# Four edits to a fused attention and MLP kernel: QK tiles cut at chunk borders, whole-tile stores, reciprocals on VectorE, and a new TensorE order

## The chip, the core and the metric

The kernel runs on one core of a Trainium2 chip. TensorE (PE) multiplies, VectorE (DVE) and ScalarE (ACT) empty the PSUM banks and do the elementwise work, GpSimd (POOL) does small elementwise work and issues the loads of inputs, and SyncE (SP) issues the DMAs that move data inside the chip's on-core memory and the stores of results. The metric is the device time of one execution in microseconds (us), here of three runs of the kernel before, and of one execution that the profiler recorded.

## The reference

Inputs are q, k, v of shape 8 batches x 12 heads x 448 tokens x 64, two 12 x 12 matrices that mix heads, and the two MLP weights (768 x 2048 and 2048 x 768).

```python
scores = scale * np.matmul(q, k.transpose(0, 1, 3, 2))
scores = np.einsum('bhij,hg->bgij', scores, w_pre)
attn = np.exp(scores - np.max(scores, axis=-1, keepdims=True))
attn = attn / (np.sum(attn, axis=-1, keepdims=True) + 1e-09)
attn = np.einsum('bhij,hg->bgij', attn, w_post)
x = np.matmul(attn, v)            # heads side by side: 3584 x 768
h = np.maximum(x @ w_in, 0.0)
return h * h @ w_out
```

## The kernel before

**Chunks and tiles.** Mixing heads contracts over heads, so for one token all 12 heads have to lie on partitions. A chunk is 10 tokens of one batch with 12 heads, 120 rows, in two groups of 60 (5 tokens each). A batch has 45 chunks (the last one has 8 tokens and is moved as two pieces of 4). The scores q k^T are made in QK tiles of many tokens, one head per PSUM bank (`emit_QK`, line 955), emptied into `stage` (two slots, tokens on partitions), and carried from there by DMAs on SP into `dring`, a ring of 16 chunk slots with heads and tokens on partitions (`emit_rel`, line 1023). A chunk that crosses the border of two QK tiles needs two of these DMAs. QK tiles are 128, 128, 128 and 64 tokens; the tile of 64 is multiplied for two pairs of heads at once, so that it needs 3 TensorE units and not 6.

For the first 30 chunks of batch 0 there is a direct way without `stage`: q is spread with zeros in `qz`, and units `spr` write scores with heads and tokens already on partitions. The other 148 tokens of batch 0 are two QK tiles.

**Softmax.** Units `pre` mix the heads of a pair of chunks (`emit_pre`, line 1045). ACT takes the exponent, with the sum of each row in `rowsum` (line 1094). Then `rec` (line 1109 on) writes the reciprocals of a pair's row sums to `rinv`: on DVE with the reciprocal instruction for the first five pairs, on POOL as a power of minus one for the other 179 (line 1117, `minus1` is its exponent). `fold` multiplies them into the second mixing matrix (`wk2s`, line 1127, on POOL after the first five pairs). Units `post` (line 1159) mix the exponents with `wk2s` into the transposed second scores, which DVE or ACT copies to `a2t`. Units `avq` and `av` multiply with v (lines 1216, 1237) into `xt`. The no-max form of softmax is checked at the end: after the last exponent, DVE tests all row sums, SP turns the answer round by a DMA, and a flag is made (`t_flag`).

**MLP.** Units `h` (`emit_F1`, line 1275) multiply by w_in, ACT or DVE takes the positive part, DVE squares into `h2t`. Units `o` (`emit_F2`, line 1406) multiply 128 result rows by w_out. The rows are emptied into `osb` (two slots) and stored by DMAs on SP (line 1473): one per piece of `pieces_of`, two pieces of 64 rows for nearly all tiles, since the rows of `h2t` are even and odd groups of tokens that lie apart in the output. The last two tiles store half rows each as soon as it is there (`emit_last`, line 1366).

**What sets the order.** The program is written out whole by a planner (`_Plan`). The order of TensorE's units is the string ORDER, one character a unit: the position of the character in CODES, divided by ten, gives the form (0, 1, 2), and the remainder the stream (0 transposes, 1 QK, 2 pre, 3 post, 4 av, 5 direct units, 6 and 7 `h`, 8 and 9 `o`) from which the next unit is taken. The form is how the 128 x 128 array is split: `row` (two halves of 64 rows at once), `quad` (four 64 x 64 blocks), `full`, `cols`, `c32`. Units `h` and `o` can run in any of row, full and quad; in `row` and `quad` both banks of a pair are filled together over two units, in `full` one after the other. The other four engines' tasks are put in order by the planner from its costs: FETCH (an instruction block's arrival), DMA times, and a cost for each task. An eviction that may run on ACT or DVE goes to the one that the planner expects to be done first. Each engine then runs its list in order and waits on semaphores.

**The end.** `emit_engine` (line 1624): each engine runs its list, waits for the flag, loads it into a register (line 1631) and branches (line 1632): when a row sum was out of range everything is done again with the maximum taken off. SP waits for its stores (`final`, line 1574) only behind that branch.

Of the kernel before, what the change touches and what calls it, by code (L numbers as in the profile page):

```python
# [7 lines left out]
ALU = mybir.AluOpType  # L8
DT = mybir.dt
# [3 lines left out]
ACT = "act"  # L13
DVE = "dve"
POOL = "pool"
SP = "sp"
# [3 lines left out]
MODE_SWITCH = 100.0  # L20
ACT_BIAS = 14.5
BLOCK = 256
FETCH = (2700.0, 2300.0, 1500.0)
EVENTS = {"tr": 0.12, "qk": 0.72, "di": 0.2, "sp": 0.3, "po": 0.61, "pr": 1.1, "av": 0.43, "o0": 0.43}
DMA_START = {"move": 2590.0, "load": 2640.0, "big": 1680.0}
DMA_AHEAD = 1600.0
DMA_END = {"move": 1450.0, "load": 1300.0}
INF = float("inf")
CODES = "0123456789abcdefghijklmnopqrst"
ORDER = (  # L30
    "0000511100551155555555555555555c2155555035bcb02515525353c2c5155c1531333355c2555c355332c0"
    "240443c4b200gh1111h62b3g33hqc31cgc3h2b3hgh3bbbch3633r3gb42444223g1h72qgqb2733g1r12q713h3"
    "6b2673722392003t122j33t2b282bi338333s04202444bb002gqbb28311i313s111s322gh2227hqh3613q1hr"
    "3363q2422444br2br631q1731h613q32h0220gh22qg373r3c38212i3s333814144420022ghh20028118111i1"
    "33s339b22j31t22193229119313t3319242444312q2bq227373163c3631731h2020q1g2br2h236333q20b0r2"
    "r20038318311i33184bb42244229c19311t133t118222833i313s242444232q2b623713733631g12r2br2006"
    "33q33rb17q200262r217293c3t331t2200jc181118133s311842244422391319313t13392422444222838333"
    "i311i31qb2b62qb2622h73733373q1b6rb00h2q0202q22h700239331911j11193182238318331s2424442228"
    "1s311i333814244413bq22g2rb2r23631q32r2br23633g31r002h2633q733r024044412tb2j0209bb2t23811"
    "381138333s11t22jb2922t23831s33i1318b4244422bq2bqb27337631q33731r2q21q2r22h1633673373bs22"  # L40
    "842i2i244422383833s333s22qr6r22293933t33tq4q444hghh6gq7g6hrghisrggh7hg7giqishhjjijtsttsj"
    "j"
)


# [327 lines left out]
def bass_talking_heads_attention__then__ffn_squared_relu_kernel(  # L373
# [10 lines left out]
    B, H, S, D = q.shape  # L384
# [4 lines left out]
    NR = CH * H  # L389
    NCH = -(-S // CH)  # L390
    IT = 128
    ND = 30
    NE = 6
    NQ0 = 2
    QT0 = tuple((CH * (ND + x * (NCH - ND) // NQ0),
                 min(S, CH * (ND + (x + 1) * (NCH - ND) // NQ0))) for x in range(NQ0))
    QT = tuple((i, min(S, i + IT)) for i in range(0, S, IT))
    NP = H // 2
    PJ = 64
    NT = S // PJ  # L400
# [15 lines left out]
    with ExitStack() as es:  # L416
        def sb(name, shape, dtype):
            return es.enter_context(nc.sbuf_tensor(name, list(shape), dtype))
# [29 lines left out]
        goods = sb("goods", [1, 128], DT.float32)  # L448
        flag = sb("flag", [1, 1], DT.int32)
        rinv = sb("rinv", [128, NPS, 1], DT.float32)  # L450
        minus1 = sb("minus1", [128, 2, 1], DT.float32)
        sb("align", [128, 64], DT.uint8)
        w_in_sb = sb("w_in_sb", [128, NFT, FF], DT.bfloat16)
        w_out_sb = sb("w_out_sb", [128, NFFT, F], DT.bfloat16)
# [38 lines left out]
        def program(guard):  # L493
# [9 lines left out]
            def add(name, engine, fn, deps, cost, prio, mode=None, group=None, instrs=0):  # L503
                return plan.add(name, engine, fn, deps, cost, prio, "ctr", 1, mode, group=group,
                                instrs=instrs)
# [28 lines left out]
            def fn_init(eng, en):  # L534
                eng.memset(mask[:, :, :], 1.0)
                eng.memset(wk1[:, :], 0.0)
                eng.memset(wrep[:, :], 0.0)
                eng.memset(wrepf[:, :], 0.0)
                eng.memset(maskf[:, :], 0.0)
                eng.memset(wkf[:, :, :], 0.0)  # L540
                eng.memset(wk2b[:, :, :], 0.0)
                eng.memset(rowsum[:, NCP - 1::NCP, :], 1.0)
                eng.memset(minus1[:, :, :], -1.0)
                return eng.memset(ident[:, :], 0.0)

            t_init = add("init", DVE, fn_init, [], {DVE: (950.0, 1050.0)}, -3e6)
# [476 lines left out]
            def emit_rel(b, c, n, r0, d0, nv):  # L1023
                g = b * NCP + c
                slot = g % NDS
                sem = sem_dsx[c // (IT // CH) - 1] if d0 else sem_dsl[slot]

                def fn(eng, en):
                    o = R0 + d0 * H
                    eng.dma_start(dring[o:o + nv * H, slot, :],  # L1030
                                  stage[r0:r0 + nv, n % 2, :, :]).then_inc(sem.handle, 16)

                t = plan.add("rel%d_%d_%d" % (b, c, d0), SP, fn, sev_of[n],
                             {SP: (1000.0, 0.0)}, g * 1.0, sem, 16,
                             dma=("move", 10.0 + 73.3 * nv, 54.0))
                rel.setdefault(g, []).append(t)
                rel_of[n].append(t)
# [48 lines left out]
            def after_pre(g, t_pre, gr, x):  # L1086
# [26 lines left out]
                p0 = g0 % NPS  # L1113

                def fn_rec(eng, en):
                    if en == POOL:
                        return eng.tensor_tensor(rinv[:, p0:p0 + n, :], rowsum[:, g0:g0 + n, :],  # L1117
                                                 minus1[:, 0:n, :], ALU.pow)
                    return eng.reciprocal(rinv[:, p0:p0 + n, :], rowsum[:, g0:g0 + n, :])

                t_rec = add("rec%d_%d" % (b, c), DVE if g < 10 else POOL, fn_rec,
                            [exp_of[g0], t_exp] + old_users(g),
                            {DVE: (82.0, 160.0), POOL: (120.0, 180.0)}, b * 1000.0 - 900 + c)

                def fn_fold(eng, en):
                    i0 = wk2b[:, :, :].rearrange("p a b -> p (a b)").unsqueeze(1)
# [279 lines left out]
            def emit_F2(b, tile, s, s_F):  # L1406
# [58 lines left out]
                    if hh == 0:  # L1465
                        f.early.append(t_oe)
                pieces = pieces_of(b, tile)

                o_free[s] = []
                for x, (p0, n_p, row, step) in enumerate(pieces):  # L1470
                    def fn_od(eng, en, p0=p0, n_p=n_p, row=row, step=step):
                        dst = bass.AP(out.tensor, row * F, [[step * F, n_p], [1, F]])
                        eng.dma_start(dst, osb[p0:p0 + n_p, s, :]).then_inc(sem_out[s].handle, 16)

                    o_free[s].append(plan.add("odma%d_%d_%d" % (b, tile, x), SP, fn_od, evs,
                                              {SP: (720.0, 0.0)}, b * 1000.0 + 710, sem_out[s], 16,
                                              dma=("move", 50.0 + 12.0 * n_p, 200.0)))
                odmas.extend(o_free[s])


# [55 lines left out]
            if not guard:  # L1536
                inside = stage[:, 1, 0:2, :].rearrange("p a b -> p (a b)")[:, 0:B * NCP]
                i_ = rowsum[:, :, :].rearrange("p a b -> p (a b)")
                last_exp = [t for g, t in exp_of.items() if g >= B * NCP - NCP]
                used = [t for ts in rel.values() for t in ts]  # L1540

                def fn_in(eng, en):
                    return eng.tensor_scalar(inside, i_, 1e30, None, op0=ALU.is_lt)

                def fn_both(eng, en):
                    return eng.scalar_tensor_tensor(inside, i_, 1e-30, inside, op0=ALU.is_gt,
                                                    op1=ALU.mult)

                def fn_least(eng, en):
                    return eng.tensor_reduce(good[:, :], inside, AX.X, ALU.min)  # L1550

                def fn_turn(eng, en):
                    eng.dma_start(goods[0:1, :], good[:, 0:1]).then_inc(sem_good.handle, 16)

                def fn_flag(eng, en):
                    return eng.tensor_reduce(flag[:, :], goods[:, :], AX.X, ALU.min)

                t_in = add("good0", DVE, fn_in, list(exp_of.values()) + used,
                           {DVE: (450.0, 550.0)}, 1e8)
                t_in = add("good1", DVE, fn_both, [t_in], {DVE: (450.0, 550.0)}, 1e8)  # L1560
                t_in = add("good2", DVE, fn_least, [t_in], {DVE: (450.0, 550.0)}, 1e8)
                t_turn = plan.add("turn", SP, fn_turn, [t_in], {SP: (780.0, 2800.0)}, 1e8, sem_good, 16)
                t_flag = add("flag", DVE, fn_flag, [t_turn], {DVE: (200.0, 300.0)}, 1e8)

            for g, ts in rel.items():
                for t in ts:
# [57 lines left out]
        def emit_engine(eng_name, eng):  # L1624
            tasks = fast[eng_name]
            k = len(tasks)
            while k and tasks[k - 1].name == "final":
                k -= 1
            emit_tasks(eng_name, eng, tasks[:k], fast_waits)
            eng.wait_ge(t_flag.sem.handle, t_flag.semval)  # L1630
            fine = eng.value_load(flag[0:1, 0:1])
            with eng.If(fine == 0):
                emit_tasks(eng_name, eng, tasks[k:], fast_waits)
                for s_, v_ in reached:
                    eng.wait_ge(s_.handle, v_)
                emit_tasks(eng_name, eng, slow[eng_name], slow_waits)
            if k < len(tasks):
                with eng.Else():
                    emit_tasks(eng_name, eng, tasks[k:], fast_waits)

        with nc.Block() as block:
            @block.tensor
# [46 lines left out]
```

## Time and profile before

| | |
|---|---|
| three runs | 538.87, 530.79, 534.45 us; median 534.45 |
| the profiled execution | 531.75 us, of which its span is 530.1 |
| PE busy | 504.9 us, 95% of the span |
| ACT busy | 429.9 us, 81% |
| DVE busy | 387.7 us, 73% |
| POOL busy | 292.6 us, 55% |
| matmuls | 10519 |

The span runs from the first to the last instruction. "Busy" counts the time in which at least one instruction of an engine was under way; matmuls overlap, and the time from the start of one unit to the start of the next says more of TensorE than the duration that is printed. In a list by time, a row has the start, the time from start to end of a merged run of like instructions, engine, line, operation, tiles, and the count. In a list of groups, the columns behind the bar are the busy time, the mean duration in ns, and the idle time of the engine just before them with what ended it. In a list of waits a row reads: engine and line, the engine and line that it waited for, total us, times, longest.

### The profile page before, as it was taken

What the parts mean: (1) busy time and instruction counts of PE and PEld (TensorE: products, weight loads), DVE (VectorE), ACT (ScalarE), POOL (GpSimd) and SP (SyncE); (2) the same over time, 40 slices, a digit from 0 to 9 for tenths busy, and PEclk for the clock granted to TensorE, in tenths of its full rate; (3) what the DMA queues carried; (4) which work ended last, traced back from release to release, by engine and by line L of the source; (5) the groups of instructions that cost most, each with busy time, mean ns of one, the idle gap of its engine ahead of it and who ended that gap; (6) DMA issues with size and microseconds to landing.
All of it is one profiled execution on the core that took longest, in us unless ns stands there. A gap on an engine that the chain in (4) does not pass through costs nothing.

```text
span 530.1 us, 24988 instructions
## 1 busy us (share of the span) xinstructions
PE 504.9 (95%) x10519; PEld 329.4 (62%) x10519; DVE 387.7 (73%) x816; ACT 429.9 (81%) x1223; POOL 292.6 (55%) x524
## 2 busy tenths in 40 slices
PE   8999999999999999999899989999999999999994
PEld 4446776668765655666566655566666665678862
DVE  7898987889886699867787667776888668555400
ACT  5999989889978798888798878978978878977420
POOL 9847788527944597258752576416964445442000
PEclk9999999999999999999999999999999999999998
DMA  9999999646965799458954699536992567531022
GB/s 165 197 201 172 181 192 183 140 96 138 180 147 117 158 167 185 101 113 155 176 115 96 126 196 151 119 64 146 181 176 55 124 139 145 113 93 35 1 57 70
DMA packets 81811, 71.10 MB, mean 134 GB/s; under 512 B 13610, under 2 KB 78234, under 8 KB 81690
## 3 DMA queue, kind: packets, MB, share of 16 engines
q1 hardware_dynamic: 48138, 46.62, 36.1%
q0 software_dynamic: 33392, 22.59, 31.3%
q8 instruction: 86, 1.41, 1.1%
q14 instruction: 35, 0.29, 0.2%
q10 hardware_dynamic: 160, 0.20, 0.1%
HBM read 45.63 MB, written 11.01 MB: 107 GB/s over the span
## 4 chain that ended last, share of the span: by engine, by line
PE 72%; ACT 15%; POOL 7%; DVE 2%; issue 2%; DMA 1%; ACTq 0%; POOLq 0%
PE ps L1435 23%; PE ps L1296 13%; PE ps L1288 7%; PE ps L1159 7%; ACT pring L1094 6%; PE ps L1069 5%; PE ps L1237 5%; PE ps L985 4%; ACT stage L524 4%; POOL rinv L1117 3%; PE ps L1375 2%; PE ps L1427 2%; ACT dring L524 1%; POOL wk2s L1127 1%; PE ps L975 1%
## 5 line engine op out<-in xcount | busy, mean ns | idle before, releaser
L1117 POOL TENSOR_TENSOR rinv<-rowsum,minus 128x2 f32<-128x2 f32 (+1 forms) x179 | 126.1, 706 | 174.7 <-ACT pring L1094 173.9
L1094 ACT ACTIVATE pring<-ps 128x448 bf16<-128x448 f32 x360 | 192.3, 562 | 12.0 <-PE ps L1069 9.4
L525 DVE CAST a2t<-ps 128x480 bf16<-128x480 f32 (+1 forms) x205 | 124.8, 641 | 31.6 <-PE ps L1159 30.6
L1435 PE MATMUL ps<-w_out_sb,h2t 64*128 64x384 bf16 (+1 forms) x1728 | 141.4, 323 | 0.5 <-issue 0.4
L525 DVE CAST stage<-ps 128x448 bf16<-128x448 f32 (+1 forms) x193 | 115.0, 617 | 25.8 <-PE ps L985 15.1
L1296 PE MATMUL ps<-xt,w_in_sb 64*64 64x448 bf16 (+4 forms) x1872 | 121.0, 327 | 1.8 <-issue 1.2
L524 ACT ACTIVATE a2t<-ps 128x480 bf16<-128x480 f32 (+1 forms) x163 | 87.6, 581 | 22.5 <-PE ps L1159 21.7
L1435 PEld LDWEIGHTS ps<-w_out_sb,h2t 64*128 64x128 bf16 (+1 forms) x1728 | 74.6, 97 | 45.1 <-issue 1.9
L524 ACT ACTIVATE stage<-ps 128x448 bf16<-128x448 f32 (+1 forms) x167 | 87.0, 549 | 14.3 <-PE ps L985 9.6
L1296 PEld LDWEIGHTS ps<-xt,w_in_sb 64*64 64x64 bf16 (+1 forms) x1872 | 65.0, 102 | 34.5 <-issue 2.5
L1094 ACT ACTIVATION_READ_ACCUMULATOR pring<-ps 128x1 f32 x360 | 81.6, 227 | 0.0
L1127 POOL TENSOR_TENSOR wk2s<-wk2b,rinv 128x120 bf16<-128x120 bf16 (+1 forms) x179 | 70.7, 396 | 12.4
L1159 PEld LDWEIGHTS ps<-wk2s,pring 60*128 60x128 bf16 x2880 | 56.6, 93 | 31.9 <-DVE a2t L525 4.8
L1159 PE MATMUL ps<-wk2s,pring 60*128 60x60 bf16 x2880 | 64.8, 187 | 6.9 <-POOL wk2s L1127 4.2
L1343 DVE TENSOR_TENSOR h2t<-h1t 128x448 bf16<-128x448 bf16 (+2 forms) x176 | 53.3, 331 | 23.3 <-ACT h1t L1333 22.5
L1069 PE MATMUL ps<-dring,wk 64*64 64x448 bf16 (+1 forms) x622 | 54.5, 359 | 2.6 <-ACT h1t L1333 0.9
L1333 ACT ACTIVATE h1t<-ps 128x448 bf16<-128x448 f32 (+2 forms) x93 | 40.4, 439 | 14.4 <-PE ps L1288 5.9
L1334 DVE TENSOR_SCALAR h1t<-ps 128x448 bf16<-128x448 f32 (+2 forms) x83 | 41.3, 505 | 11.4 <-PE ps L1296 8.4
L1288 PE MATMUL ps<-xt,w_in_sb 128*128 128x220 bf16 (+2 forms) x420 | 47.4, 265 | 0.2
L1288 PEld LDWEIGHTS ps<-xt,w_in_sb 128*128 128x128 bf16 x420 | 38.2, 98 | 7.3 <-ACT pring L1094 0.9
L985 PE MATMUL ps<-qkt 64*128 64x448 bf16 (+1 forms) x288 | 39.5, 353 | 1.4 <-DVE a2t L525 0.8
L738 POOL DMA_DIRECT2D vraw<-in_v_dram x54 | 34.3, 640 | 0.0
(76 smaller groups left out, 434.2 us busy)
## 6 DMA issues: line engine op xcount, KB each, us to landing
dring<-stage SPq DMA_DIRECT2D x301, 105.0 KB
out_dram<-osb SPq DMA_DIRECT2D x45, 192.0 KB, 3.6
qraw<-in_q_dram POOLq DMA_DIRECT2D x42, 112.0 KB, 5.0
kraw<-in_k_dram POOLq DMA_DIRECT2D x42, 112.0 KB, 5.1
w_in_sb<-in_moe_w_in_dram POOLq DMA_DIRECT2D x8, 384.0 KB, 10.2
w_out_sb<-in_moe_w_out_dram POOLq DMA_DIRECT2D x8, 384.0 KB, 8.9
vraw<-in_v_dram POOLq DMA_DIRECT2D x21, 128.0 KB
vraw<-in_v_dram POOLq DMA_DIRECT2D x21, 96.0 KB
```

The lines of the kernel that those rows point to most:

```text
L524: return eng.activation(o, i_, AF.Copy)
L525: return eng.tensor_copy(o, i_)
L985: r_ = eng.matmul(ps[y * w:(y + 1) * w, g.banks[x], 0:S], qkt[r0:r0 + 64, pb, p + y, 0, i0:i0 + w], qkt[r0:r0 + 64, pb, p + y, 1, :], star ...
L1069: r_ = eng.matmul(ps[64 * y:64 * y + 64, gr.banks[x], 0:S], wk1[64 * x:64 * x + 64 - R0 * x, 64:128], dring[64 * x:64 * x + 64 - R0 * x, ( ...
L1094: return eng.activation(pring[:, pr, 0:S], ps[:, gr.banks[x], 0:S], AF.Exp, accum_out=rowsum[:, g, :])
L1117: return eng.tensor_tensor(rinv[:, p0:p0 + n, :], rowsum[:, g0:g0 + n, :], minus1[:, 0:n, :], ALU.pow)
L1127: return eng.tensor_tensor(wk2s[:, p0:p0 + n, :], i0.to_broadcast([128, n, PR]), rinv[:, p0:p0 + n, :].to_broadcast([128, n, PR]), ALU.mult)
L1159: r_ = eng.matmul(ps[:, gr.banks[x], o0:o0 + PR], pring[64 * x:64 * x + PR, pr + y, j0:j0 + 2 * PJ], wk2s[64 * x:64 * x + PR, pr + y, :], ...
L1288: r_ = eng.matmul(ps[:, g.banks[ph], 0:n], w_in_sb[:, ft, t * 128:(t + 1) * 128], xt[:, ft, c0:c1], start=(ft == 0), stop=(ft == NFT - 1))
L1296: r_ = eng.matmul(ps[z:z + w, g.banks[x], 0:n], w_in_sb[64 * y:64 * y + 64, ft, t * 128 + z:t * 128 + z + w], xt[64 * y:64 * y + 64, ft, c ...
L1343: return eng.tensor_tensor(h2t[:, t16, o0:o0 + n], h1t[:, s, 0:n], h1t[:, s, 0:n], ALU.mult)
L1435: r_ = eng.matmul(ps[z:z + w, g.banks[hh], 0:FH], h2t[64 * y:64 * y + 64, t16, col + z:col + z + w], w_out_sb[64 * y:64 * y + 64, t16, hh ...
```

## The change

1. QK tiles of batches 1 to 7 are 120, 120, 120 and 88 tokens. Each of the four is made by 6 units (the last one computes 128 rows, of which 88 are used). No chunk crosses a border, so each chunk is one DMA. In batch 0 the direct way takes 32 chunks and one QK tile of 128 tokens the rest.
2. In batches 1 to 7, two pieces of a result tile are stored by one DMA with a three-level address; the tile that joins two batches, those of batch 0 and the last two stay as they were.
3. All reciprocals are on DVE; `minus1` is gone.
4. ACT and SP take the flag and the branch in the middle of their lists, as soon as the flag is there (tasks `turnact` and `turnsp`), and have what follows written twice, behind each side of the branch.
5. The planner's costs for an instruction block (4.0 us whatever the DMAs do), for a DMA's end and for SP's issue are others, and ORDER is a new string of 986 characters in place of 969.

```diff
-FETCH = (2700.0, 2300.0, 1500.0)
+FETCH = (4000.0, 0.0, 0.0)
...
-DMA_END = {"move": 1450.0, "load": 1300.0}
+DMA_END = {"move": 1700.0, "load": 1300.0}
...
 ORDER = (
-    "0000511100551155555555555555555c2155555035bcb02515525353c2c5155c1531333355c2555c355332c0"
...
+    "0051100555500555555155555555555222555555553155311cc002c53002255531c5352335555c3525155333300"
...
-    ND = 30
+    ND = 32
     NE = 6
-    NQ0 = 2
+    NQ0 = 1
...
-    QT = tuple((i, min(S, i + IT)) for i in range(0, S, IT))
+    QT = tuple((i, min(S, i + 120)) for i in range(0, 360, 120)) + ((360, S),)
...
-                             {SP: (1000.0, 0.0)}, g * 1.0, sem, 16,
+                             {SP: (950.0, 0.0)}, g * 1.0, sem, 16,
...
                 def fn_rec(eng, en):
-                    if en == POOL:
-                        return eng.tensor_tensor(rinv[:, p0:p0 + n, :], rowsum[:, g0:g0 + n, :],
-                                                 minus1[:, 0:n, :], ALU.pow)
                     return eng.reciprocal(rinv[:, p0:p0 + n, :], rowsum[:, g0:g0 + n, :])
 
-                t_rec = add("rec%d_%d" % (b, c), DVE if g < 10 else POOL, fn_rec,
-                            [exp_of[g0], t_exp] + old_users(g),
-                            {DVE: (82.0, 160.0), POOL: (120.0, 180.0)}, b * 1000.0 - 900 + c)
+                t_rec = add("rec%d_%d" % (b, c), DVE, fn_rec, [exp_of[g0], t_exp] + old_users(g),
+                            {DVE: (82.0, 160.0)}, b * 1000.0 - 900 + c)
...
-
+                whole = b and not (b % 2 and tile == 3)
                 o_free[s] = []
-                for x, (p0, n_p, row, step) in enumerate(pieces):
+                for x, (p0, n_p, row, step) in enumerate(pieces[:1] if whole else pieces):
                     def fn_od(eng, en, p0=p0, n_p=n_p, row=row, step=step):
-                        dst = bass.AP(out.tensor, row * F, [[step * F, n_p], [1, F]])
-                        eng.dma_start(dst, osb[p0:p0 + n_p, s, :]).then_inc(sem_out[s].handle, 16)
+                        if whole:
+                            dst = bass.AP(out.tensor, row * F, [[F, 2], [step * F, n_p], [1, F]])
+                            i_ = osb[:, s, :]
+                        else:
+                            dst = bass.AP(out.tensor, row * F, [[step * F, n_p], [1, F]])
+                            i_ = osb[p0:p0 + n_p, s, :]
+                        eng.dma_start(dst, i_).then_inc(sem_out[s].handle, 16)
...
+                for en in (ACT, SP):
+                    plan.add("turn" + en, en, None, [t_flag], {en: (3600.0, 3600.0)}, -1e8)
...
-            while k and tasks[k - 1].name == "final":
-                k -= 1
+            for i, t in enumerate(tasks):
+                if t.name == "turn" + eng_name:
+                    k = i
+            rest = tasks[k + 1:]
             emit_tasks(eng_name, eng, tasks[:k], fast_waits)
             eng.wait_ge(t_flag.sem.handle, t_flag.semval)
             fine = eng.value_load(flag[0:1, 0:1])
             with eng.If(fine == 0):
-                emit_tasks(eng_name, eng, tasks[k:], fast_waits)
+                emit_tasks(eng_name, eng, rest, fast_waits)
                 for s_, v_ in reached:
                     eng.wait_ge(s_.handle, v_)
                 emit_tasks(eng_name, eng, slow[eng_name], slow_waits)
-            if k < len(tasks):
+            if rest:
                 with eng.Else():
-                    emit_tasks(eng_name, eng, tasks[k:], fast_waits)
+                    emit_tasks(eng_name, eng, rest, fast_waits)
```

More of the change, by code (lines that the diff above doesn't have):

```diff
@@ L30 @@
 ORDER = (
-    "0000511100551155555555555555555c2155555035bcb02515525353c2c5155c1531333355c2555c355332c0"
[L32 to L42, printed above, removed]
+    "0051100555500555555155555555222555555553155311cc002c53002255531c5352335555c3525155333300"
+    "5242111431244322g32qh331rg3b3h612bbhgh2b3r2226hg333g2h2424443c3h611g13gr111h622g337h7332"
+    "hqg0220hg3b2911j111t333j2040244224381001i111i13c83bbqbqbc3831c82238c12i373h33gh22237h6q3"
+    "32g4244314b22hghqb2bg7133gh22b00i3c3s333bg2r1b1h2b671363q32020g2h2gr3373r200bb8b2b8bb424"
+    "4332c8c3i111s331811224239323j323tt24b2441134332hbb22g319333t22b9020bj317bbb6g33r2002h22h"
+    "336bb002g331hbbbg222ghqb2bh333ibb28bb22j3339242444333s111832bsb2bi42244432s223823g313gbb"
+    "002t113j2b2g2373373373r0022ghbb002gbbb6133g22267b2h333h332tb2b9bbb92424442j2381183138133"
+    "814244b239222j39313931831182422i118200263363731r30022ghb0220hb2bq116333636131q2r2bhbrb22"
+    "r4244439133j24244421j113j3383s22281i138133s2200i122s6113637331r31gb22hg220000h6313q17131"
+    "h32q2b62rb2h42444223913j1139133933s2ib2s284b24443831s33i1812t2bt2b29b2j236333g711371bq22"
+    "6qb2g2713r3733h32q42q2hri22444333siigj9h2222rgt383i33833i49hg6g444ghhg7iqhg7qgsghig8qrhg"
+    "rhhhhjqsjij99ts89j"
 )
@@ L450, in bass_talking_heads_attention__then__ffn_squared_relu_kernel @@
         rinv = sb("rinv", [128, NPS, 1], DT.float32)
-        minus1 = sb("minus1", [128, 2, 1], DT.float32)
         sb("align", [128, 64], DT.uint8)
@@ L542, in fn_init @@
                 eng.memset(rowsum[:, NCP - 1::NCP, :], 1.0)
-                eng.memset(minus1[:, :, :], -1.0)
                 return eng.memset(ident[:, :], 0.0)
@@ L1467, in emit_F2 @@
                 pieces = pieces_of(b, tile)
+                whole = b and not (b % 2 and tile == 3)
                 o_free[s] = []
-                for x, (p0, n_p, row, step) in enumerate(pieces):
+                for x, (p0, n_p, row, step) in enumerate(pieces[:1] if whole else pieces):
                     def fn_od(eng, en, p0=p0, n_p=n_p, row=row, step=step):
-                        dst = bass.AP(out.tensor, row * F, [[step * F, n_p], [1, F]])
-                        eng.dma_start(dst, osb[p0:p0 + n_p, s, :]).then_inc(sem_out[s].handle, 16)
+                        if whole:
[5 more added lines that the diff above has]
+                        eng.dma_start(dst, i_).then_inc(sem_out[s].handle, 16)
                     o_free[s].append(plan.add("odma%d_%d_%d" % (b, tile, x), SP, fn_od, evs,
-                                              {SP: (720.0, 0.0)}, b * 1000.0 + 710, sem_out[s], 16,
-                                              dma=("move", 50.0 + 12.0 * n_p, 200.0)))
+                                              {SP: (900.0 if whole else 720.0, 0.0)},
+                                              b * 1000.0 + 710, sem_out[s], 16,
+                                              dma=("move", 50.0 + 12.0 * n_p * (2 if whole else 1),
+                                                   200.0)))
                 odmas.extend(o_free[s])
```

## The prediction

> **What bounds the kernel now.** I read the page's busy times and chain first, then TensorE's list by time, then the waits.
>
> ```profile
> span 530.1 us, 24988 instructions
> ...
> PE 504.9 (95%) x10519; PEld 329.4 (62%) x10519; DVE 387.7 (73%) x816; ACT 429.9 (81%) x1223; POOL 292.6 (55%) x524
> ...
> PE 72%; ACT 15%; POOL 7%; DVE 2%; issue 2%; DMA 1%; ACTq 0%; POOLq 0%
> ```
>
> TensorE is busy for 95% of the span and is 72% of the chain that ended last. So the end moves with what TensorE has to do and with the gaps between its units. The list by time, PE alone, shows both:
>
> ```profile
> 111.71 0.39 PE L1159 MATMUL ps<-wk2s,pring 60*128 60x60 bf16 x16
> 111.93 0.35 PE L985 MATMUL ps<-qkt 64*128 64x448 bf16 x2
> 112.13 0.39 PE L1159 MATMUL ps<-wk2s,pring 60*128 60x60 bf16 x16
> 112.35 1.46 PE L1435 MATMUL ps<-w_out_sb,h2t 64*128 64x384 bf16 x16
> 113.65 0.73 PE L985 MATMUL ps<-qkt 64*128 64x448 bf16 x6
> 114.22 1.46 PE L1435 MATMUL ps<-w_out_sb,h2t 64*128 64x384 bf16 x16
> 115.52 0.39 PE L1159 MATMUL ps<-wk2s,pring 60*128 60x60 bf16 x16
> 115.83 0.57 PE L1069 MATMUL ps<-dring,wk 64*64 64x448 bf16 x8
> 116.34 1.30 PE L1288 MATMUL ps<-xt,w_in_sb 128*128 128x220 bf16 x12
> 117.57 0.76 PE L1069 MATMUL ps<-dring,wk 64*64 64x448 bf16 x10
> ```
>
> Take differences of starts. Where the form stays `row` (111.71 to 115.52), a `post` takes 0.22, an `o` unit 1.30, three QK units 0.57, so 0.19 for a pass of 448 columns, and nothing lies between. Where the form changes, about 0.1 comes on top: 0.31 for a `post` of 0.22 (row, then quad), 0.51 for two `pre`, each one such pass (quad, then full), and 1.23 for two full `h` units that should take 1.13 (then quad). Where that 1.13 is from, and the two ends of TensorE's work:
>
> ```profile
> 194.66 1.30 PE L1296 MATMUL ps<-xt,w_in_sb 64*128 64x448 bf16 x12
> 195.79 0.39 PE L1159 MATMUL ps<-wk2s,pring 60*128 60x60 bf16 x16
> ...
> 5.29 0.95 PE L833 MATMUL ps<-ident,qraw 64*64 64x64 bf16 x28
> ...
> 514.39 7.96 PE L1375 MATMUL ps<-w_out_sb,h2t 128*128 128x384 bf16 x48
> ```
>
> An `h` unit of 448 tokens takes 1.13; two full ones of 220 tokens stream about as many columns. Now the account. Units: 112 `o` x 1.30 = 145.6; 128 `h` of 448 tokens' worth x 1.137 = 145.5; 434 passes of 448 columns in QK, `pre` and direct units x 0.19 = 82.5; `post`, 180 pairs' worth, x 0.22 = 40; attention times v, per half batch 22 passes of some 224 columns, half of 0.19 each, so 2.08, x 16 = 33.3; transposes, 48 units of 0.24 (the last two rows under rival B), 12. Together 459. Walking ORDER character by character, each stream's units in the order in which they are made, I count 216 changes of form: x 0.11 = 23.8. The first real unit starts at 5.3 and the last ends at 514.39 + 7.96 = 522.4. What is left, **34 us** (522.4 - 5.3 - 459 - 23.8), is TensorE standing still. 7.7 us of the span lie behind its end, and 1.65 outside the span (531.75 - 530.1).
>
> **The change, part by part.**
>
> *Work.* Seven batches have 24 QK units in place of 21, batch 0 has 6 in place of 12: 15 more. Two more direct chunks are 4 passes, and the other forms of `pre` take one off. 18 x 0.19 = **+3.4**.
>
> *Form.* The new ORDER has 307 changes, 91 more, since 148 of the `h` and `o` units are `full` against 78: 91 x 0.11 = **+10.0**. It also has 9826 matmuls in place of 10502 (10519 less 17 warm-ups), because `full` does with one matmul what `row` does with two.
>
> *Standing still.* 13.4 us have to be won back from the 34. What the waits name:
>
> ```profile
> PE ps L1159 <- POOL wk2s L1127: 4.2, 5, 1.3
> ...
> PEld ps L1159 <- POOL wk2s L1127: 1.2, 2, 0.7
> ...
> POOL rinv L1117 <- ACT pring L1094: 173.9, 62, 8.2
> ```
>
> ```profile
> L1117 POOL TENSOR_TENSOR rinv<-rowsum,minus 128x2 f32<-128x2 f32 (+1 forms) x179 | 126.1, 706 | 174.7 <-ACT pring L1094 173.9
> ...
> L1119 DVE RECIPROCAL rinv<-rowsum 128x2 f32<-128x2 f32 x5 | 0.8, 152 | 0.0
> ```
>
> `post` waits 5.4 for POOL. A pair's reciprocals take 706 ns there and 152 on DVE, so the way from exponent to `post` is 0.55 shorter 179 times, and POOL falls from 293 to 167 busy. I take the 5.4 as gone; what is late next is the eviction of `post`'s banks. DVE gets 179 x 0.152 = 27.2.
>
> ```profile
> L525 DVE CAST stage<-ps 128x448 bf16<-128x448 f32 (+1 forms) x193 | 115.0, 617 | 25.8 <-PE ps L985 15.1
> L524 ACT ACTIVATE stage<-ps 128x448 bf16<-128x448 f32 (+1 forms) x167 | 87.0, 549 | 14.3 <-PE ps L985 9.6
> ```
>
> Evictions: the last tile has 12 before and after (64 partitions then, 128 now, the same row); batch 0 loses 12 and gets 2 for direct chunks: -10 x 0.58 = -5.8 on two engines. DVE ends near 388 + 27 - 3 = 412, 78%: covered on the average, not in batch 0, where the engines are full:
>
> ```profile
> 20.00:40.00 20.00, 19.08 (x392) 7.80 (x384) 18.55 (x42) 20.00 (x63) 10.56 (x18) 1.00 1.16 200
> ...
> 480.00:500.00 20.00, 20.00 (x284) 17.32 (x279) 9.40 (x33) 11.04 (x28) 0.99 (x3) 1.00 0.10 23
> ```
>
> (Columns: length, then busy time of PE, PEld, DVE, ACT, POOL, clock, DMA share, GB/s.) ACT has no idle time from 20 to 40 us and DVE 1.45. So the new order can't remove the start's share. I put a floor of 5 under the standing still, an estimate: PE's idle time in that window, 0.9, and some 4 for loading and the rest of batch 0. The ceiling is 34 - 5.4 = 29, all that isn't POOL's. No row of before shows a new order; I take the **middle, 17**, and keep both ends for the range.
>
> *SP.* By count, 23 chunk DMAs and 20 stores are not issued.
>
> ```profile
> L1030 SPq DMA_DIRECT2D dring<-stage x359: 667/825/2033, 29.3 to 465.4; - x180
> ```
>
> That is 23 x 0.83 plus 20 shorter ones, some 32 us of SP's time. No matmul's wait names one of these transfers, so I cost it at nothing: TensorE's own work hides it. The bytes are the same; a store of a whole tile lands at best when half a tile does now and at worst when the second of two does, and its slot is needed only two tiles on.
>
> *The end.* Answers on the lines of flag load, branch, last wait and closing, SP and ACT:
>
> ```profile
> L1631 ACTq TENSOR_LOAD <-flag x1: 1121/1121/1121, 523.4 to 523.4; - x1
> L1631 SPq TENSOR_LOAD <-flag x1: 972/972/972, 524.1 to 524.1; - x1
> ...
> L1632 SPq COMPARE_BRANCH  x1: 50/50/50, 525.1 to 525.1; - x1
> ...
> L1574 SPq EVENT_SEMAPHORE  x2: 17/22/28, 528.3 to 528.4; - x2
> ...
> L1641 ACTq EVENT_SEMAPHORE  x1: 17/17/17, 530.0 to 530.0; - x1
> ...
> DMA to landing us min/median/max: 2.1/2.5/4.2
> ```
>
> SP's branch is at 525.1 and its next instruction at 528.3: 3.2 us in which the stores have landed anyway (the last was issued near 523.5, so about 526). With the branch taken early the wait ends about 526.3: **-2.0**, bounds 0 and -3.3 (closing at once). Early, ACT pays 1.1 + 3.2 near 485 us, ahead of its evictions; DVE is idle for half of 480 to 500 and takes them. Uncovered it costs up to 4.3; I take 0. SP's pause delays stores alone.
>
> *Sum.* 5.3 + 459 + 3.4 + 307 x 0.11 (33.8) + 17 = 518.5; tail 7.7 - 2.0 = 5.7; outside 1.65: 525.9 against its own 531.75. The median of the runs lies 2.7 above that execution, so 528.6, about **529**. Each us of standing still is one us of time: 2% faster than 534.45 (below 523.8) needs it under 12, 2% slower (over 545.1) needs 33, as much as today. Two per cent is about what a measurement of this kernel can tell from no change.
>
> **Rivals.** *A, standing still nearly goes* (5 to 12): 517 to 524. For it: a `post` that waits for POOL and what queues behind are named; against: batch 0. *B, it stays* (25 to 33), because the stops aren't of reciprocals or order; the change then doesn't do what it should: 537 to 545. For it speaks a stop inside one unit, 25 transposes of 28 and then a gap:
>
> ```profile
> 105.09 0.38 PE L837 MATMUL ps<-ident,qraw 64*64 64x64 bf16 x25
> 106.00 0.22 PE L837 MATMUL ps<-ident,qraw 64*64 64x64 bf16 x3 [0.53 <-issue]
> 106.01 0.43 PE L837 MATMUL ps<-ident,kraw 64*64 64x64 bf16 x28
> 106.25 0.38 PE L1069 MATMUL ps<-dring,wk 64*64 64x448 bf16 x4
> ```
>
> No semaphore lies there, so neither evictions nor POOL can be its cause; fewer matmuls may thin such stops by 6% only (676 of 10502). [...]
>
> *C, slower: DVE's queue.* A reciprocal waits for two exponents, and DVE's next evictions stand behind it; TensorE waits for their banks. POOL bore 173.9 us of such waiting in 62 times, harmlessly. If 0.2 us falls before each of the 179, that is 36 of DVE's time; if half reaches TensorE, 18 come on top of 17, the standing still is 35, and the time 547. It decides from 32 us of waiting before the reciprocals. Against it: the planner sets a reciprocal where it expects both exponents done, and the five on DVE show 0.0 idle.
>
> **Chances.** Forecast (12 to 25, so 524 to 537) 0.52, A 0.18, B 0.18, C 0.12. Hence faster 0.18, same 0.70, slower 0.12. The range, 518 to 543, holds the forecast, 0.15 of A and 0.14 of B, together 0.81; it leaves out C and the far ends of the two others.
>
> **What would show it.** TensorE's row: x9826 and warm-ups, `row` to `full` differences of 0.1 on top. Post no longer waits for `wk2s` on POOL; DVE near 412 with little idle time ahead of its reciprocals, SP with 336 chunk DMAs. TensorE's last matmul near 518.5 and the span's end within 6 of it, SP's branch near 485. I am wrong if the standing still, worked out as above, is under 12 or over 25, or if the tail stays at 7.7.

## The result, and the profile after

The changed kernel takes 596.88 us (median of four runs, 592.85 to 597.68) against 534.63 for the kernel before beside it: a ratio of 1.118, with a 95% interval from 1.109 to 1.126. The forecast was 529, between 518 and 543. Some 62 us have to be found.

First the page of the changed kernel: span, busy times, the clock in 40 slices, and the chain that ended last.

```profile
span 595.9 us, 23524 instructions
...
PE 530.0 (89%) x9847; PEld 329.9 (55%) x9847; DVE 392.8 (66%) x984; ACT 429.1 (72%) x1223; POOL 167.8 (28%) x345
...
PEclk9997999999999969997989987999779998999998
...
PE 66%; DMA 22%; ACT 5%; DVE 3%; SPq 2%; issue 1%; POOL 1%; DVEq 0%; ACTq 0%
PE ps L1282 13%; PE ps L1429 12%; DMA dring<-stage 10%; DMA out_dram<-osb 10%; PE ps L1290 8%; PE ps L1421 6%; PE ps L1153 6%; PE ps L1067 5%; PE ps L1231 5%; PE ps L983 3%; PE ps L973 3%; ACT pring L1092 2%; DMA kraw<-in_k_dram 2%; SPq L1028 2%; PE ps L835 1%
```

Before, TensorE was idle for 530.1 - 504.9 = 25 us; now for 65.9. DMA was 1% of the chain and is 22%. And the granted clock, 0.996 on average before and 0.951 now, has dips all over the span. By the page's lines of that chain, the stores `out_dram<-osb` have 10% of the span and the chunk DMAs `dring<-stage` another 10%. Which of them holds the others up stands in the groups and in the list of waits:

```profile
L523 ACT ACTIVATE osb<-ps 128x384 f32<-128x384 f32 x35 | 17.2, 492 | 69.5 <-DMA out_dram<-osb 46.1
...
L524 DVE COPY osb<-ps 128x384 f32<-128x384 f32 x21 | 11.7, 557 | 64.5 <-DMA out_dram<-osb 57.6
...
out_dram<-osb SPq DMA_DIRECT2D x20, 384.0 KB
```

```profile
DVE osb L524 <- DMA out_dram<-osb: 57.6, 6, 16.9
ACT osb L523 <- DMA out_dram<-osb: 46.1, 6, 13.5
...
PEld ps L983 <- ACT osb L523: 13.7, 1, 13.7
```

The evictions of results into `osb` wait for the stores that empty it, up to 16.9 us at a time. Twenty of the stores now carry a whole tile of 384 KB. One such stop by time, SP first (start, time from the first to the end of the last, count):

```profile
384.36 26.09 SPq L1028 DMA_DIRECT2D dring<-stage  x21
410.56 2.05 SPq L1472 DMA_DIRECT2D out_dram<-osb  x2
414.00 21.51 SPq L1028 DMA_DIRECT2D dring<-stage  x12
435.62 0.61 SPq L1472 DMA_DIRECT2D out_dram<-osb  x1
```

```profile
411.45 0.56 DVE L524 COPY osb<-ps 128x384 f32<-128x384 f32 x1
...
419.38 1.30 PE L1290 MATMUL ps<-xt,w_in_sb 64*128 64x448 bf16 x12
...
433.30 0.49 ACT L523 ACTIVATE osb<-ps 128x384 f32<-128x384 f32 x1 [13.50 <-DMA out_dram<-osb]
433.31 0.56 DVE L524 COPY osb<-ps 128x384 f32<-128x384 f32 x1 [13.84 <-DMA out_dram<-osb]
...
434.01 0.93 PE L983 MATMUL ps<-qkt 64*128 64x448 bf16 x4 [13.33 <-DVE osb L524]
...
435.13 2.45 PE L1290 MATMUL ps<-xt,w_in_sb 64*128 64x448 bf16 x12
...
439.98 1.31 PE L1290 MATMUL ps<-xt,w_in_sb 64*128 64x448 bf16 x12
```

Two stores are issued from 410.56 on. The next evictions into `osb` go ahead at 433.3, some 21 us after the second of them. ACT and DVE both stand at the head of their lists with such an eviction, so nothing else leaves PSUM either; TensorE finishes the `h` unit of 419.38 and stands still for 13.33 us. Then the same kind of `h` unit takes 2.45 us instead of 1.31: the granted clock is at half (0.50) from 425.0, some 4 us into the stop, to 438.7. TensorE's *busy* time is larger with these stores too: 530.0 us at a mean clock of 0.951, against 514.6 at 0.993 without them (the first run below). SP suffers as well: 12 chunk DMAs, issued one right behind the other, take 21.5 us of it, the longest 4.7; without these stores the median of one is 0.9.

What the engines of the DMA do in stretches in which hardly anything but stores of results is under way (columns as in the prediction: length, PE, PEld, DVE, ACT, POOL, clock, DMA share, GB/s), the changed kernel first and then the kernel before:

```profile
565.00:580.00 15.00, 15.00 (x118) 11.36 (x117) 2.93 (x11) 5.54 (x14) 0.00 (x0) 1.00 0.16 49
```

```profile
516.00:518.00 2.00, 2.00 (x15) 1.20 (x13) 0.00 (x0) 0.00 (x0) 0.00 (x0) 1.00 0.77 197
```

A tile in two stores keeps 0.77 x 16 = 12 engines busy and moves at 197 GB/s. Whole-tile stores keep 0.16 x 16 = 2.6 busy, at 49 GB/s. The records of the single packets say it more sharply. A tile is 128 packets of 3072 bytes in both kernels. Where little else is under way, they land in 1.7 to 2.4 us in two stores of 64 rows, for about half of that time 16 of them at once (in busier stretches in up to some 5 us); in one store they take 17.8 us of engine time in 8.7 to 9.0 us, for 8.1 of 9.0 us exactly two at once. When two such stores overlap, 256 packets take 16 to 20 us, still about two at a time.

The new address is `[[F, 2], [step * F, n_p], [1, F]]`. Its outermost count is 2, with two packets at once; that of the old one was 64, with sixteen at once for about half of the time. That the count makes the difference, and not the size of a store or the third level of its address, these two kernels don't show. The runs below test it with other counts.

### The profile page after: what moved, and what is told of

Read it like the earlier page. It is cut to its first block, busy times and chain, and to the rows that moved or that the text cites. A ratio compares the mean times of both kernels' runs of the same rounds, so it can differ in the third digit from the quotient of the medians.

```text
span 595.9 us, 23524 instructions
## 1 busy us (share of the span) xinstructions
PE 530.0 (89%) x9847; PEld 329.9 (55%) x9847; DVE 392.8 (66%) x984; ACT 429.1 (72%) x1223; POOL 167.8 (28%) x345
## 4 chain that ended last, share of the span: by engine, by line
PE 66%; DMA 22%; ACT 5%; DVE 3%; SPq 2%; issue 1%; POOL 1%; DVEq 0%; ACTq 0%
PE ps L1282 13%; PE ps L1429 12%; DMA dring<-stage 10%; DMA out_dram<-osb 10%; PE ps L1290 8%; PE ps L1421 6%; PE ps L1153 6%; PE ps L1067 5%; PE ps L1231 5%; PE ps L983 3%; PE ps L973 3%; ACT pring L1092 2%; DMA kraw<-in_k_dram 2%; SPq L1028 2%; PE ps L835 1%
## 5 line engine op out<-in xcount | busy, mean ns | idle before, releaser
L524 DVE CAST stage<-ps 128x448 bf16<-128x448 f32 x183 | 108.2, 616 | 31.2 <-PE ps L983 20.5
L1429 PE MATMUL ps<-w_out_sb,h2t 64*128 64x384 bf16 (+1 forms) x1472 | 116.1, 332 | 0.0
L1282 PE MATMUL ps<-xt,w_in_sb 128*128 128x220 bf16 (+2 forms) x720 | 105.1, 296 | 0.1
L523 ACT ACTIVATE stage<-ps 128x448 bf16<-128x448 f32 x165 | 85.5, 561 | 18.5 <-PE ps L983 14.1
L1282 PEld LDWEIGHTS ps<-xt,w_in_sb 128*128 128x128 bf16 x720 | 66.0, 99 | 30.5 <-issue 9.2
L1429 PEld LDWEIGHTS ps<-w_out_sb,h2t 64*128 64x128 bf16 (+1 forms) x1472 | 60.9, 101 | 36.3 <-issue 4.6
L1290 PE MATMUL ps<-xt,w_in_sb 64*64 64x448 bf16 (+4 forms) x912 | 67.9, 334 | 0.0
L523 ACT ACTIVATE osb<-ps 128x384 f32<-128x384 f32 x35 | 17.2, 492 | 69.5 <-DMA out_dram<-osb 46.1
L1337 DVE TENSOR_TENSOR h2t<-h1t 128x448 bf16<-128x448 bf16 (+2 forms) x176 | 53.9, 328 | 18.5 <-ACT h1t L1327 17.9
L1114 DVE RECIPROCAL rinv<-rowsum 128x2 f32<-128x2 f32 (+1 forms) x184 | 29.0, 158 | 32.7 <-ACT pring L1092 31.6
L983 PE MATMUL ps<-qkt 64*128 64x448 bf16 x198 | 33.4, 374 | 13.9 <-DVE osb L524 13.3
```

The costliest lines, as they stand in the source:

```text
L523: return eng.activation(o, i_, AF.Copy)
L524: return eng.tensor_copy(o, i_)
L983: r_ = eng.matmul(ps[y * w:(y + 1) * w, g.banks[x], 0:S], qkt[r0:r0 + 64, pb, p + y, 0, i0:i0 + w], qkt[r0:r0 + 64, pb, p + y, 1, :], star ...
L1282: r_ = eng.matmul(ps[:, g.banks[ph], 0:n], w_in_sb[:, ft, t * 128:(t + 1) * 128], xt[:, ft, c0:c1], start=(ft == 0), stop=(ft == NFT - 1))
L1290: r_ = eng.matmul(ps[z:z + w, g.banks[x], 0:n], w_in_sb[64 * y:64 * y + 64, ft, t * 128 + z:t * 128 + z + w], xt[64 * y:64 * y + 64, ft, c ...
L1337: return eng.tensor_tensor(h2t[:, t16, o0:o0 + n], h1t[:, s, 0:n], h1t[:, s, 0:n], ALU.mult)
```

## The experiments

Theory S: the store's shape is the whole loss. Rivals: the new order and its 91 further changes of form; the reciprocals in DVE's queue (rival C of the prediction); that larger stores or stores with three-level addresses are slow whatever their counts.

### The whole change without the store

```diff
-                whole = b and not (b % 2 and tile == 3)
+                whole = False
```

> The kernel after, but each result tile is stored by two DMAs of 64 rows again, as before; tiles, reciprocals, early branch and the new order stay. Theory S (spread: a store whose outermost dimension counts 2 runs on two DMA engines only; the packets of one whole-tile store took 17.8 us of engine time in 8.7 us, before 24 us in about 2): the 62 us go, 520 to 540 us, and the waits for out_dram<-osb vanish. Theory D (DVE's queue blocked by reciprocals) and theory O (the new order itself is bad): the stores were only late because others were, and the time stays over 580 us.

535.42 us against 531.25 beside it, ratio 1.0066 (1.0023 to 1.0109). Its page, and a stretch of its stores:

```profile
span 531.2 us, 23543 instructions
...
PE 514.6 (97%) x9847; PEld 325.1 (61%) x9847; DVE 391.0 (74%) x982; ACT 428.4 (81%) x1225; POOL 167.3 (31%) x345
...
PE 86%; ACT 6%; DMA 5%; issue 1%; POOL 1%; SPq 0%; DVE 0%; ACTq 0%; POOLq 0%
```

```profile
520.00:522.00 2.00, 2.00 (x14) 1.17 (x12) 0.00 (x0) 0.00 (x0) 0.00 (x0) 1.00 0.77 195
```

The span falls from 595.9 to 531.2: 49.3 of the 64.7 us are idle time of TensorE (65.9 against 16.6) and 15.4 are its busy time (530.0 against 514.6), for the same 9847 matmuls. Of the waits for the stores this is left:

```profile
DVE osb L524 <- DMA out_dram<-osb: 2.0, 2, 1.8
ACT osb L523 <- DMA out_dram<-osb: 1.6, 2, 1.4
```

The rest of the change is within 1.1% of the kernel before, and on the slower side.

### The store alone

The kernel before with part 2 of the change; its order and its planner's costs of blocks and chunks stay as they were; the planner is told of the larger store, as in the changed kernel.

```diff
+                whole = b and not (b % 2 and tile == 3)
...
+                for x, (p0, n_p, row, step) in enumerate(pieces[:1] if whole else pieces):
...
+                            dst = bass.AP(out.tensor, row * F, [[F, 2], [step * F, n_p], [1, F]])
```

> The kernel before, with the whole-tile store alone (order, tiles, reciprocals as before). Theory S: slower by 30 to 65 us, 565 to 600 us, with evictions into osb that wait for out_dram<-osb for 50 us or more. Theories D and O: 525 to 540 us, since neither reciprocals nor order are changed.

597.34 us, ratio 1.126 (1.117 to 1.135). The span is 595.2, and the same waits lead:

```profile
DVE osb L525 <- DMA out_dram<-osb: 50.8, 8, 19.9
ACT osb L524 <- DMA out_dram<-osb: 22.1, 4, 8.5
```

So the store makes the loss in either order, with QK tiles of either kind, and without a reciprocal having moved.

### The count instead of the size

Two kernels tell the shape from the rest. In both, each store of 64 rows of the same tiles is cut in two along its rows, with plain two-level addresses as before: into 62 and 2 rows in one, into 56 and 8 in the other. The number of transfers and of bytes is the same in both; only the outermost counts differ (62 and 2, against 56 and 8).

```diff
+                if b and not (b % 2 and tile == 3):
+                    pieces = [q for p0, n_p, row, step in pieces
+                              for q in ((p0, 62, row, step), (p0 + 62, n_p - 62, row + 62 * step, step))]
```

> The kernel before, with each store of 64 rows cut into one of 62 and one of 2 rows: twice as many stores on SP, none larger than before. If a store is spread over as many of the 16 DMA engines as divide its outermost count, both go on two engines: Theory S expects 550 to 600 us. If what hurts is the size of one store (384 KB) or its three-level address, nothing of that is here: 530 to 545 us.

> The kernel before, with each store of 64 rows cut into 56 and 8: as many stores as with 62 and 2, but 56 has a divisor of 14 and 8 one of 8, so 14 and 8 engines. Theory S (engines by the divisor of the outermost count): 528 to 542 us, no different from before. If the number of stores or SP's time for them was what cost 78 us with 62 and 2: 580 us and more.

62 and 2: 609.72 us, ratio 1.149 (1.140 to 1.159). 56 and 8: 543.36 us, ratio 1.023 (1.019 to 1.028). Each was executed twice. The waits of the first for its stores:

```profile
ACT osb L524 <- DMA out_dram<-osb: 49.3, 12, 10.3
DVE osb L525 <- DMA out_dram<-osb: 36.5, 10, 7.1
```

In the second no wait for `out_dram<-osb` is left. A stretch of little but stores, in the first and then in the second:

```profile
592.00:602.00 10.00, 2.03 (x13) 1.00 (x11) 0.00 (x0) 0.00 (x0) 0.00 (x0) 0.79 0.24 68
```

```profile
528.00:530.00 2.00, 2.00 (x15) 1.21 (x13) 0.00 (x0) 0.00 (x0) 0.00 (x0) 1.00 0.65 197
```

With 62 rows to a store, 128 packets took 17.9 us of engine time in 9.6 us: two at once again, though the store is smaller than the old one and its address has two levels. With 56 they landed in 1.7 us, most often 14 at once, where the old stores of 64 rows had 16. So with outermost counts of 2, 62, 56 and 64 the packets at once were, most of the time, 2, 2, 14 and 16: at these four, the largest number up to 16 that divides the count. In these runs neither a larger transfer nor a three-level address is the cause; the count is. The second kernel is still 12 us slower than before, just above what was expected of it. It issues 40 more DMAs on SP than the kernel before, and TensorE is idle for 34.0 us in place of 25.2; which of them cost it that is open.

### The reciprocals alone

```diff
-                t_rec = add("rec%d_%d" % (b, c), DVE if g < 10 else POOL, fn_rec,
+                t_rec = add("rec%d_%d" % (b, c), DVE, fn_rec,
```

> The kernel before, with all reciprocals on DVE alone, at the old order. Theory S: within 2% of before, 527 to 542 us; by my prediction's term the post waits for POOL (5.4 us) go and 27 us of DVE come, so about 530 us. Theory D: DVE's evictions stand behind reciprocals, over 550 us.

530.10 us, ratio 0.9991 (0.9952 to 1.003): no difference. The group and its wait:

```profile
L1119 DVE RECIPROCAL rinv<-rowsum 128x2 f32<-128x2 f32 (+1 forms) x184 | 28.8, 157 | 26.5 <-ACT pring L1094 25.9
```

```profile
DVE rinv L1119 <- ACT pring L1094: 25.9, 37, 1.6
```

DVE does wait ahead of the reciprocals, 25.9 us in 37 times, near the point from which rival C was to decide, and none of it shows in the time. `post` hardly waits for POOL any more: of its two rows of 4.2 and 1.2 us the first is gone and the second is 0.7. But the time didn't fall by those 4.7 us either.

### The early branch alone, and with the reciprocals

Part 4 of the change in the kernel before, in its order; then the same with the reciprocals on DVE as in the experiment above.

```diff
+                for en in (ACT, SP):
+                    plan.add("turn" + en, en, None, [t_flag], {en: (3600.0, 3600.0)}, -1e8)
...
+            for i, t in enumerate(tasks):
+                if t.name == "turn" + eng_name:
+                    k = i
+            rest = tasks[k + 1:]
...
```

> The kernel before, with the early branch on ACT and SP alone. My prediction's term: 2.0 us less (bounds 0 and 3.3), so a ratio near 0.996; with two stores in place of the whole-tile store, the new order's run had 4.6 us behind TensorE's last matmul in place of 7.7, so 3 us less is to be expected of this part. Rival: ACT's pause near 485 us reaches TensorE and eats it, ratio 1.000 or more.

> The kernel before, with reciprocals on DVE and the early branch, the two parts that cost nothing by themselves: old order, old tiles, two stores. Reciprocals alone gave 0.999; with 2 to 3 us from the early branch 0.993 to 0.997, about 529 us. If the parts don't add up, 0.999 or more.

The branch alone: 528.44 us, ratio 0.9948 (0.9917 to 0.9979). Both: 525.85 us, **ratio 0.9887 (0.9855 to 0.992)**, the fastest kernel here, about 1% below the kernel before. Of the second, the page, ACT by time, and SP's last wait:

```profile
span 522.0 us, 24982 instructions
...
PE 504.3 (97%) x10519; PEld 327.2 (63%) x10519; DVE 402.6 (77%) x998; ACT 426.9 (82%) x1220; POOL 168.2 (32%) x345
```

```profile
484.91 0.35 ACT L1333 ACTIVATE h1t<-ps 128x220 bf16<-128x220 f32 x1 [4.02 <-DVE h2t L1343]
```

```profile
L1576 SPq EVENT_SEMAPHORE  x2: 17/22/28, 519.5 to 521.5; - x2
```

ACT pays its 4 us at 481 to 485; TensorE is busy without a gap from 478 to 488, so nothing of it reaches TensorE. TensorE ends at 518.5 and the span 3.5 behind it (7.7 before).

### The tiles alone

QK tiles of 120, 120, 120 and 88 in the kernel before, with the old order, in which each unit of the last tile becomes two (form `quad`), so that the changes of form stay 216.

```diff
-    QT = tuple((i, min(S, i + IT)) for i in range(0, S, IT))
+    QT = tuple((i, min(S, i + 120)) for i in range(0, 360, 120)) + ((360, S),)
```

> The kernel before, with QK tiles of 120, 120, 120 and 88 in batches 1 to 7 alone; in its order each unit of the old 64-token tile becomes two units one behind the other, in the form of their neighbours, so the changes of form stay 216. The sum's term for this: 21 units x 0.19 = 4.0 us more, ratio 1.007. If the 21 chunk DMAs that are no longer issued were worth something, it is below 1.004; if the order suffers from the longer units beyond their own time, above 1.012.

536.94 us, ratio 1.0084 (1.0049 to 1.0119), which is 4.5 us. The chunk DMAs fall to 338, and no time comes back for it: the interval leaves out both the less than 1.004 and the more than 1.012 that were named.

### Stops without a semaphore

Without the store, the changed kernel has one stop of 3.62 us that no semaphore explains. TensorE by time:

```profile
42.18 0.56 PE L914 MATMUL ps<-qkt,h2t 128*32 128x448 bf16 x8
46.37 0.90 PE L1052 MATMUL ps<-dring,wkf 128*128 128x448 bf16 x2 [3.62 <-issue]
```

It falls on an instruction whose number is 193 modulo 256, counted from 0 in TensorE's list (weight loads, matmuls and waits on semaphores). In eight traces (both given kernels, this one, the reciprocals alone, the branch alone, both, and the two shifted kernels), every stop over 0.4 us that no semaphore explains falls on that number. To move it, in this kernel the first warm-up matmuls (10 of 448 columns) were replaced by 60 of 64 columns, which adds about 100 instructions ahead of everything:

```diff
+                m, w = (6 * n, 64) if now < 3000.0 else (n, S)
...
-                    for _ in range(n):
+                    for _ in range(m):
```

> The kernel after with two stores per tile, and TensorE's ten warm-up matmuls of 448 columns at the start replaced by sixty of 64 columns: about 100 more instructions before the first real one, the same time. TensorE then stood still for 3.8 us at 46.3 us, at an instruction whose number is 193 modulo 256, as several others in this and other runs. [...] Theory W (it waits for data or a bank): the same `pre` unit stops for the same 3.8 us near 46 us, and the ratio stays 1.007.

```profile
41.74 0.28 PE L836 MATMUL ps<-ident,qraw 64*64 64x64 bf16 x10 [0.19 <-ACT a2t L523]
44.71 0.47 PE L836 MATMUL ps<-ident,qraw 64*64 64x64 bf16 x18 [2.70 <-issue]
```

537.35 us, ratio 1.0107 (1.0069 to 1.0146): not faster. But the stop, 2.70 us here, moved from a `pre` unit into the middle of a transpose unit, to the instruction that now is number 193 modulo 256. So it hangs on the place in the instruction list and not on the work. Most of the places with that number show no stop: in the kernel before, 8 of 84 show a stop of TensorE over 0.15 us that no semaphore explains, in the changed one without its store 4 of 79, in the fastest one 10 of 84. These add up to 4.3, 5.6 and 5.9 us. (The larger figure in the expectation, 3.8 us for this stop, doesn't come out as idle time.) What TensorE waits for at these places isn't shown.

The fastest kernel with the same edit of the warm-up:

> The kernel before with reciprocals on DVE, the early branch, and the sixty short warm-up matmuls in place of ten long ones. With two of those three its ratio was 0.989. [...] A ratio under 0.985 would make it the fastest version.

528.50 us, ratio 0.9921 (0.9883 to 0.9959): no better than unshifted (0.9887). Here too the shift gained nothing.

## Why the prediction was wrong, by its own steps

**The step that failed is *SP*.** It said of the twenty stores: "I cost it at nothing: TensorE's own work hides it", and "a store of a whole tile lands at best when half a tile does now and at worst when the second of two does, and its slot is needed only two tiles on". The bytes were counted and the address was not. With an outermost count of 2 the tile lands after 9 to 20 us instead of 1.7 to 5, `osb` has two slots, and both evicting engines stand behind them. That costs 596.88 - 535.42 = 61 us in the new order and 597.34 - 531.25 = 66 us in the old one. That no wait named the stores was true of the kernel before, where they landed in time, and said nothing of later stores. With two packets at once assumed, an estimate was to be had from the trace of before: a tile took about 24 us of engine time there, so some 12 us two at a time (alone it was 9, beside another such store 20). Against a tile of results every 19 us on the average (530 us for 28 tiles), and tiles that come in bunches, that isn't hidden.

**Without that step** the forecast can be held against the kernel with two stores. Its profiled execution took 532.99 us where the sum said 525.9; its runs' median is 535, inside the range, but on the other side of the kernel before: about 1% faster was forecast, and it is 0.7% slower. The end of its last matmul comes from this row, 518.59 + 7.96 = 526.6:

```profile
518.59 7.96 PE L1369 MATMUL ps<-w_out_sb,h2t 128*128 128x384 bf16 x48
```

- *Standing still* was the mis-sized term. By the prediction's own sum it is 526.6 - 5.2 (the first unit) - 462.4 - 33.8 = 25 us, where 17 was taken from between 5 and 29, and 34 was there before. That is 8 us too little. Only part of this remainder is TensorE standing still: between the first unit and the last matmul the profile has 16.0 us of idle time before and 10.5 here; in the rest TensorE counts as busy for longer than the sum's prices of units and form changes give. Rival B's reason was half right: the stops inside the list of instructions exist, and here they are 5.6 of the 10.5. The largest, 3.62, is at 46 us, and the granted clock is at half from 45.6 to 52.4.
- *Work*, 3.4, wasn't measured as a whole. Of its parts the tiles alone cost 4.5 us, where 4.0 was expected.
- *Form*: 307 changes and 9826 matmuls (9847 less 21 warm-ups) came as counted. What the order as a whole is worth was not measured by itself. By subtraction (1.0066 for everything without the store, 0.9887 for reciprocals and branch) tiles, direct chunks and order cost 1.8%, of which the tiles alone measured 0.84; the remainder is argued, not shown.
- *The end*: the tail was to shrink from 7.7 us to 5.7. In the kernel with two stores it is 4.6. The branches and SP's last wait:

```profile
L1637 SPq COMPARE_BRANCH  x1: 50/50/50, 486.0 to 486.0; - x1
```

```profile
L1577 SPq EVENT_SEMAPHORE  x2: 17/22/28, 527.7 to 530.7; - x2
```

  SP branches at 486.0, where 485 was said, and the end now goes by the landing of the last store. The branch alone measured 2.8 us (0.5%).
- *Reciprocals*: 4.7 of the 5.4 us of waiting for POOL went, nearly as said; by itself that gave no time. Together with the branch 1.1% went, against 0.5% by the branch alone, and with these intervals the two may still simply add up. What took the 4.7 us up when the reciprocals moved alone is open. In its one profiled execution the stops at 193 modulo 256 come to 7.2 us, where they were 4.3 before; moved stops may have taken it, which one execution doesn't show.
- *Rival C* is refuted at its own place: 25.9 us of waiting ahead of the reciprocals, half of which should have reached TensorE, and a ratio of 0.9991. (In the changed kernel without its store it is 30.7.) *DVE near 412* was too high: 391 and 399.9. Instructions of DVE overlap at their ends (those before last 428.6 us one by one, in 387.7 us of busy time), so 28 us more of reciprocals made its busy time only 12 longer.
- *Chunk DMAs*: 336, as counted. Their issues, in the changed kernel and then with two stores (shortest, median, longest in ns, first and last start):

```profile
L1028 SPq DMA_DIRECT2D dring<-stage x336: 673/934/10967, 29.5 to 526.0; - x168
```

```profile
L1028 SPq DMA_DIRECT2D dring<-stage x336: 682/903/1916, 29.1 to 462.9; - x168
```

  SP's relief, 32 us by the prediction, was worth nothing, as said; it was the single issue of up to 10.97 us, beside slow stores, that no step had.

No rival held the slower side by this mechanism. The chance of 0.12 for slower belonged to DVE's queue alone.

## What to carry to other kernels

When a DMA's address changes, read its outermost count before counting transfers and bytes: in these runs, where little else was under way, two stores of 64 rows landed in about 2 us what one store with an outermost count of 2 landed in 9 (20 beside another such store), and cuts of 56 and 8 rows were 66 us better than cuts of 62 and 2. A store that is "off the path" is so only as long as its buffers come free: price the wait of the engine that refills the buffer. And try a bundle's parts alone: two of these edits together take 1.1% off, inside a bundle that loses 12%.

## What was not expected of the hardware

- TensorE paid twice for the stops behind slow stores. In the stretch of the stop shown above the mean clock was 0.66 (last columns: clock, DMA share, GB/s):

```profile
420.00:440.00 20.00, 6.67 (x104) 3.74 (x102) 4.55 (x10) 3.80 (x9) 0.97 (x2) 0.66 0.54 110
```

  An `h` unit took 2.45 us right behind it and 1.31 some 5 us later. Over the whole run TensorE's busy time was 15.4 us longer than with two stores, for the same matmuls, beside 49.3 of idle time; the mean clock was 0.951 against 0.993.
- Beside slow stores, some of SP's issues of other DMAs took longer: one issue of a chunk DMA took 10.97 us, where 1.92 is the longest with two stores (the medians are 0.93 and 0.90).
- TensorE stopped, for up to 3.62 us at a time, at places of its instruction list that lie 256 instructions apart, though at most of these places it didn't stop (8 of 84 before, 4 of 79 with two stores, 10 of 84 in the fastest kernel). Where the list was shifted, the stop of 3.62 us at 46.4 became one of 2.70 at 44.7, at the same number, 193 modulo 256, and inside another unit.
